# Reversing the query-tile order of every second key tile in the values product of an attention kernel

## The chip, the cores and the metric

The kernel runs on one core of a Trainium2 chip, so no other core of this program competes with it. The metric is the time of one execution on the device in microseconds (us); the median of several runs is quoted. The granted clock is the share of its full speed that TensorE was allowed; a run with a lowered clock would be slow. Times of a kernel are compared with runs of the kernel before on the same chip, made in the same rounds.

## The reference, cut to what matters

The computation is one attention block with 32 heads over a cached key and value store, gated by a SwiGLU network:

```python
xn = _layernorm(x)
q = (xn @ wq).reshape(B, Sq, H, Dh)              # Sq = 2048, H = 32, Dh = 192
scores = einsum("bhqd,bhkd->bhqk", q, k_cache) * Dh ** -0.5   # Sk = 2048
p = _softmax(scores)
o = einsum("bhqk,bhkd->bhqd", p, v_cache)        # the "values" product
s = o.reshape(B, Sq, H * Dh) @ wo
g = _silu(w2 of (silu(xn @ w1) * (xn @ w3)))
return x + s * g
```

(Shortened and re-laid; the change touches the line of `o` only.)

## The kernel before: the parts that matter

The attention is a stream of 1024 units: 32 heads x 4 blocks of 512 queries x 8 pairs of key tiles. For each unit the kernel computes the transposed scores of 256 keys and 512 queries (`st2`), takes the exponential on ScalarE into `pT2` (bf16), and multiplies by the values. The scores of unit n + 2 are issued just ahead of the values of unit n, so ScalarE has time for its work. (The code is shortened, and its comments are added here; `p` counts the 8 pairs of key tiles.)

```python
for n, (h, qb, p) in enumerate(stream):
    ...
    scores(n + 2)
    values(n)
    ...

def emit_scores(h, qb, p):          # three rounds, two row halves each
    ...
    for r, (ka, qa, kb, qb2) in enumerate(rounds):
        nc.tensor.matmul(st2[:, 0:512], lhsT=ka, rhs=qa, ...)       # rows 0..63
        nc.tensor.matmul(st2[:, 512:1024], lhsT=kb, rhs=qb2, ...)   # rows 64..127
    pT2 = pp.tile([P, 1024], BF16, tag="pT2", name="pT2")
    nc.scalar.activation(out=pT2[:], in_=st2[:], func=ACT.Exp, scale=att_scale)

vts = [vtp.tile([P, NKT, DH + 2], BF16, name=f"vt{i}") for i in range(2)]   # DH = 192

def values(n):
    h, qb, p = stream[n]
    if p == 0:
        for r in range(2):
            obanks[r] = ps_o.tile([P, 1024], F32, tag=f"ob{r}", name=f"obank{r}")
    ...
    for t in range(2):              # key tile of the unit
        for j in range(4):          # query tile of the block
            start = p == 0 and t == 0 and j % 2 == 0
            stop = p == NPAIR - 1 and t == 1 and j % 2 == 1
            for r in range(2):      # row half: keys 0..63 and 64..127 of the tile
                nc.tensor.matmul(obanks[r][:, j * 256:j * 256 + DH + 1],
                                 lhsT=pT2[r * 64:(r + 1) * 64, t * 512 + j * P:t * 512 + (j + 1) * P],
                                 rhs=vt[r * 64:(r + 1) * 64, 2 * p + t, 0:DH + 1], start=start, stop=stop)
    if p < NPAIR - 1:
        return
    ...
    nc.vector.tensor_copy(out=osum[:], in_=ov[0])
    nc.vector.tensor_tensor(out=osum[:], in0=osum[:], in1=ov[1], op=ALU.add)
```

Each matmul uses 64 of the 128 rows of the array, and the two row halves `r` write two different accumulators, `obank0` and `obank1`. An accumulator holds four query tiles, 256 fp32 columns apart; the kernel starts and stops query tiles 0 and 1 together and 2 and 3 together, and each such half of an accumulator (512 columns) is called a bank below. And a row of the values tile `vt` has 194 elements, 388 bytes, of which 193 are streamed (192 values and a column of ones that gives the softmax denominator).

## Time and profile before

| | before |
|---|---|
| time, first 3 runs | 1942.03 us (1940.68 to 1942.1) |
| profiled span | 1938.7 us, clock 0.999 |
| TensorE busy (PE) | 1929.6 us |
| ScalarE, VectorE busy | 61%, 34% |
| share of the values matmuls in the chain that ended last | 35% |

These are lines of the page of the kernel before: busy time by engine, the chain of work that ended last, and two groups of instructions. A group's columns are line, engine, operation, destination<-sources, shapes and count; then busy us and mean ns of one; then the idle time of the engine before them and what ended it. PE is TensorE's matmuls and PEld its weight loads, DVE is VectorE, ACT ScalarE and POOL GpSimd.

```profile
PE 1929.6 (100%) x27273; PEld 1318.5 (68%) x27281; DVE 654.0 (34%) x997; ACT 1180.2 (61%) x1278; POOL 282.6 (15%) x501
...
PE obank L516 35%; PE st L487 33%; PE ps L424 14%; PE ps_s L111 11%; PE ps_f L727 3%; PE ps_gu L701 1%; PE st L488 1%; DVE stats L316 0%; PE ps L410 0%; DMA x_all<-in_A_x_dram 0%; DVE xn L346 0%; PE ps L391 0%; PE pst L354 0%; DVE mv L317 0%; PE pk L271 0%
...
L516 PE MATMUL obank<-vt,pT 64*128 64x193 bf16 x16384 | 851.8, 243 | 0.0
...
L525 DVE COPY osum<-obank 128x772 f32<-128x772 f32 x128 | 123.0, 961 | 788.9 <-PE obank L516 788.9
```

PE is busy throughout and the values matmuls never wait (0.0 us of idle time before 16384 of them). "Mean 243 ns" is the length of one record, from start to a modelled end; records overlap, so it is not the pace. The pace is in the starts. This is the timeline of TensorE of the kernel before, one unit long; its columns are start us, length us, then engine, line, operation and count.

```profile
901.26 0.38 PE L487 MATMUL st<-qA,KW 64*128 64x512 bf16 x1
901.27 0.38 PE L488 MATMUL st<-qC,KW 64*128 64x512 bf16 x1
901.48 0.38 PE L487 MATMUL st<-qC,KW 64*128 64x512 bf16 x1
901.48 0.38 PE L488 MATMUL st<-qA,KW 64*128 64x512 bf16 x1
901.70 0.38 PE L487 MATMUL st<-qC,KW 64*128 64x512 bf16 x1
901.70 0.38 PE L488 MATMUL st<-qB,KW 64*128 64x512 bf16 x1
901.91 0.83 PE L516 MATMUL obank<-vt,pT 64*128 64x193 bf16 x16
902.58 0.38 PE L487 MATMUL st<-qA,KW 64*128 64x512 bf16 x1
```

The two row halves start together (901.26 and 901.27), a pair every 0.22 us for 512 columns, and the 16 values matmuls take from 901.91 to 902.58. And these are TensorE's waits of the kernel before (waiter and what it waited for: total us, times, longest us); they add up to 3.5 us in the whole run.

```profile
PE pk L569 <- POOL ident_bf masks.py:199: 2.8, 1, 2.8
PE st L487 <- ACT pT L490: 0.3, 1, 0.3
PE pst L354 <- DVE xn L346: 0.2, 1, 0.2
PE st L483 <- DVE qA L393: 0.2, 1, 0.2
```

For finer reading, the starts of single matmuls were taken from the trace and averaged over all values units that stand unmixed in it (some 1020 of 1024). A "step" is the time from the start of one pair to the start of the next. The "unit period" is the median from the start of one unit's scores to the start of the next unit's.

| kernel | steps 1 to 7 between the 8 pairs, ns | unit period, ns |
|---|---|---|
| before | 83.3, 83.3, 83.3, 83.3, **87.5**, 82.5, 82.5 | 1316 |

The fifth step, which is the time that the fifth pair takes, is 4 ns longer than its neighbours in every unit. It is called the bump below: the fifth pair is the first of the second key tile.

### The profile page before, as it was taken

How to read it: one execution, taken by the hardware profiler on the slowest of the kernel's cores; microseconds unless marked ns; L12 is line 12 of the kernel's file. 1: busy time of each engine (PE TensorE's matmuls, PEld its weight loads, DVE VectorE, ACT ScalarE, POOL GpSimd, SP SyncE). 2: the span in 40 equal slices, each digit the busy share in tenths (PEclk: the TensorE clock that was granted, in tenths of full speed). 3: DMA queues.
4: the chain of work that ended last, by engine and by line, in shares of the span. 5: the costliest groups of instructions: out<-in, count | busy, mean ns of one | idle time of the engine just before them, and what ended most of it. 6: DMA issues, size and time to landing. Idle time of an engine off the chain costs nothing.

```text
span 1938.7 us, 59672 instructions
## 1 busy us (share of the span) xinstructions
PE 1929.6 (100%) x27273; PEld 1318.5 (68%) x27281; DVE 654.0 (34%) x997; ACT 1180.2 (61%) x1278; POOL 282.6 (15%) x501
## 2 busy tenths in 40 slices
PE   9999999999999999999999999999999999999998
PEld 6666666666666666666666666666666666577776
DVE  7333333333333333333333333333333334521111
ACT  6677676767676767776767777677767677210000
POOL 3111111111111111111111111111111110000000
PEclk9999999999999999999999999999999999999999
DMA  7643433323233433353434333434333220937772
GB/s 181 129 101 67 98 68 86 83 60 88 59 89 62 99 62 98 68 162 68 101 65 100 68 101 68 101 64 100 69 71 94 57 69 2 262 67 135 152 152 61
DMA packets 394643, 178.98 MB, mean 92 GB/s; under 512 B 341616, under 2 KB 382832, under 8 KB 394384
## 3 DMA queue, kind: packets, MB, share of 16 engines
q1 hardware_dynamic: 371136, 125.32, 30.3%
q0 software_dynamic: 19472, 45.71, 9.6%
q8 instruction: 215, 3.52, 0.8%
q10 hardware_dynamic: 3776, 4.06, 0.6%
q14 instruction: 44, 0.36, 0.1%
HBM read 52.82 MB, written 27.79 MB: 42 GB/s over the span
## 4 chain that ended last, share of the span: by engine, by line
PE 98%; DVE 1%; DMA 0%; ACT 0%; issue 0%; POOL 0%; DVEq 0%; ACTq 0%
PE obank L516 35%; PE st L487 33%; PE ps L424 14%; PE ps_s L111 11%; PE ps_f L727 3%; PE ps_gu L701 1%; PE st L488 1%; DVE stats L316 0%; PE ps L410 0%; DMA x_all<-in_A_x_dram 0%; DVE xn L346 0%; PE ps L391 0%; PE pst L354 0%; DVE mv L317 0%; PE pk L271 0%
## 5 line engine op out<-in xcount | busy, mean ns | idle before, releaser
L490 ACT ACTIVATE pT<-st 128x1024 bf16<-128x1024 f32 x1024 | 1046.2, 1022 | 251.8 <-PE st L488 236.2
L516 PEld LDWEIGHTS <-pT 64*128 64x128 bf16 x16384 | 713.7, 94 | 242.2 <-ACT pT L490 0.2
L516 PE MATMUL obank<-vt,pT 64*128 64x193 bf16 x16384 | 851.8, 243 | 0.0
L487 PE MATMUL st<-qC,KW 64*128 64x512 bf16 x2046 | 605.6, 376 | 0.1
L525 DVE COPY osum<-obank 128x772 f32<-128x772 f32 x128 | 123.0, 961 | 788.9 <-PE obank L516 788.9
L488 PE MATMUL st<-qB,KW 64*128 64x512 bf16 x1024 | 385.0, 376 | 0.0
L487 PE MATMUL st<-qA,KW 64*128 64x512 bf16 x1022 | 384.3, 376 | 0.4 <-ACT pT L490 0.3
L488 PE MATMUL st<-qC,KW 64*128 64x512 bf16 x1022 | 384.3, 376 | 0.0
L488 PE MATMUL st<-qA,KW 64*128 64x512 bf16 x1022 | 384.3, 376 | 0.0
L487 PEld LDWEIGHTS <-KW 64*128 64x128 bf16 x3068 | 278.0, 94 | 153.8 <-issue 2.1
L424 PE MATMUL ps<-xnT,W 64*128 64x512 bf16 x1280 | 297.2, 376 | 0.0
L424 PE MATMUL ps<-xnS,W 64*128 64x512 bf16 x1280 | 296.3, 376 | 0.0
L488 PEld LDWEIGHTS <-KW 64*128 64x128 bf16 x3068 | 278.0, 94 | 0.7 <-issue 0.6
L377 POOL DMA_DIRECT2D qC<-qA x124 | 65.4, 528 | 1285.6 <-DVE rl_all L532 1270.0
L430 ACT CAST qB<-ps 128x512 bf16<-128x512 f32 x131 | 76.7, 586 | 228.5 <-PE ps L424 222.9
L111 PE MATMUL ps_s<-wo_sb,oT 128*128 128x384 bf16 (+3 forms) x1535 | 208.8, 299 | 0.1
L424 PEld LDWEIGHTS <-W 64*128 64x128 bf16 x2560 | 122.9, 94 | 121.2
L111 PEld LDWEIGHTS <-oT 128*128 128x128 bf16 x1536 | 148.4, 98 | 60.4
L526 DVE TENSOR_TENSOR osum<-osum,obank 128x772 f32<-128x772 f32 x128 | 122.7, 958 | 13.4
L533 DVE TENSOR_TENSOR ostage<-osum,rl_all 128x768 bf16<-128x768 f32 x128 | 122.6, 958 | 4.4
L465 DVE SCALAR_TENSOR_TENSOR hT<-pt,qB 64x512 bf16<-64x512 bf16 x64 | 43.8, 684 | 199.5 <-ACT pt L464 199.5
L429 DVE CAST qA<-ps 128x512 bf16<-128x512 f32 x131 | 90.5, 691 | 25.2 <-PE ps L410 7.3
(84 smaller groups left out, 623.8 us busy)
## 6 DMA issues: line engine op xcount, KB each, us to landing
o_scr<-ostage SPq DMA_DIRECT2D x16, 1536.0 KB, 10.0
vt<-in_A_v_cache_dram SPq DMA_DIRECT2D x63, 384.0 KB, 5.6
qC<-qA POOLq DMA_DIRECT2D x248, 64.0 KB, 1.9
qC<-qB POOLq DMA_DIRECT2D x124, 64.0 KB, 2.3
wo_sb<-in_A_wo_dram POOLq DMA_DIRECT2D x1, 7680.0 KB, 35.3
W<-in_A_wq_dram POOLq DMA_DIRECT2D x32, 160.0 KB, 3.4
W<-in_B_w_dram POOLq DMA_DIRECT2D x32, 80.0 KB, 3.1
W<-in_A_wq_dram POOLq DMA_DIRECT2D x32, 80.0 KB, 2.9
```

What stands on the lines that cost most here:

```text
L111: nc.tensor.matmul(ps[:, 0:w], lhsT=oT[:, k, :], rhs=wo_sb[:, k, c0:c1], start=(k == 0), stop=(k == OC - 1))
L377: nc.gpsimd.dma_start(out=qC[0:64, half, :], in_=qAB[half][64:P, :])
L424: nc.tensor.matmul(ps[:, r * 512:(r + 1) * 512], lhsT=W[rows, j, :], rhs=xs[rows, j // 2, qs], start=(j == 0), stop=(j == 2 * DC - 1))
L429: a = nc.vector.tensor_copy(out=qAB[0][:], in_=ps[:, 0:512])
L430: b = nc.scalar.copy(out=qAB[1][:], in_=ps[:, 512:1024])
L487: nc.tensor.matmul(st2[:, 0:512], lhsT=ka, rhs=qa, start=r == 0 and nr == 3, stop=r == nr - 1)
L488: nc.tensor.matmul(st2[:, 512:1024], lhsT=kb, rhs=qb2, start=r == 0 and nr == 3, stop=r == nr - 1)
L490: nc.scalar.activation(out=pT2[:], in_=st2[:], func=ACT.Exp, scale=att_scale)
L516: nc.tensor.matmul(obanks[r][:, j * 256:j * 256 + DH + 1], lhsT=pT2[r * 64:(r + 1) * 64, t * 512 + j * P:t * 512 + (j + 1) * P], rhs=vt[r ...
L525: nc.vector.tensor_copy(out=osum[:], in_=ov[0])
L526: nc.vector.tensor_tensor(out=osum[:], in0=osum[:], in1=ov[1], op=ALU.add)
L533: nc.vector.tensor_tensor(out=ostage[:, qb * 4:qb * 4 + 4, hg * DH:(hg + 1) * DH], in0=osum[:, :, 0:DH], in1=rl.unsqueeze(2).to_broadcast( ...
```

## The change

The intent to be read from the diff: walk the second key tile's query tiles backwards, so that the middle of a unit stays on the same query tile and the same accumulator columns, and the accumulator bank changes twice in a unit instead of four times over a unit and its seam. The `stop` flag moves with the last matmul of each bank.

```diff
         for t in range(2):
-            for j in range(4):
+            for j in (range(4), range(3, -1, -1))[t]:
                 start = p == 0 and t == 0 and j % 2 == 0
-                stop = p == NPAIR - 1 and t == 1 and j % 2 == 1
+                stop = p == NPAIR - 1 and t == 1 and j % 2 == 0
                 for r in range(2):
                     nc.tensor.matmul(obanks[r][:, j * 256:j * 256 + DH + 1],
```

## The prediction

> **What bounds the kernel now.** TensorE. The page gives PE 1929.6 us of 1938.7 us busy, and the chain of waits that ended last is 98% PE: 35% on the values matmuls (obank), about 34% on the scores matmuls (st), 14% on the projections (ps), 11% on the output products. The granted clock is 0.999. Nothing keeps PE waiting in the attention stage: its waits total about 3.4 us, nearly all before the first head; the 16384 values matmuls have 0.0 us of idle time before them.
>
> A values unit is 16 matmuls, 64 rows x 193 columns, issued as 8 pairs (two row halves, two accumulator tiles). From the starts of single matmuls in the trace: 3.4 ns between the halves of a pair, about 80 ns to the next pair, 669.0 ns per unit. The Trainium skill, "TensorE: Matmul & The Clock Gate", section "Back-to-back issue gap", gives columns / 2.4 + 2.5 ns, which for 193 is 82.9 ns, or 663 ns for 8 pairs. The trace agrees to within 6 ns a unit: the unit is bound by streaming 193 columns per pair, and no order can shorten that.
>
> **What the change removes, adds and moves.** Comparing the instruction lists of both kernels, every engine has the same number, sequence and waits. In the second key tile of each unit, weights and accumulator columns are walked 3,2,1,0 instead of 0,1,2,3. Each query tile still adds its key tiles in the same order, so the result is bit-equal. Removed: 0 us. Added: 0 us. Weights are loaded for every matmul before and after: no reload is saved.
>
> New is that in the middle of a unit two consecutive pairs add to the same accumulator columns. Would that stall? This trace says no: the output products add to one address in chains of 48, at 162 ns (384 columns), 109 ns (256) and 56 ns (128, in the last tile). 56 ns is shorter than the 83 ns between the two pairs here.
>
> One irregularity: the step from the fifth pair to the sixth takes 84 ns instead of 80 in every unit. If the reversal removed it, 4 ns x 1024 units = 4 us (0.2%) would go; if it doubled it, 4 us would come. I expect it to stay where it is, at the first pair of the second key tile, because that is where the streamed operand changes, in both orders.
>
> The evictions wait for the last matmul of a block in either order, so they do not move.
>
> **Share on the critical path.** All of the values work (35%), but its length does not change.
>
> **Prediction: 1942.0 us, range 1937 to 1947.** Chances: faster by over 2% 0.01, within 2% 0.97, slower by over 2% 0.02.
>
> **What would show each step.** Starts of single matmuls: 669 ns per unit, with the middle step (fourth to fifth pair) still 80 ns, and the bump at the same place. Chain shares: obank 35% again. Values matmul mean 243 ns, busy about 852 us.
>
> **What would make it wrong.** A stall when the row-half mode adds twice running to the same columns: every 10 ns at that point would cost 10 us in total (1024 units); 2% needs a stall of 38 ns. Or the bump being tied to the address of weights or accumulator rather than to the streamed operand, worth about 4 us either way.

## The result, and the profile after

The kernel after took 1941.35 us (median of 6 runs, 1941.08 to 1942.05) and the kernel before 1941.95 us (6 runs, 1940.68 to 1942.1). The ratio is 0.9999 with a 95% interval of 0.9986 to 1.0012: the same. (Here and below a ratio is the mean time of one kernel's fast runs over that of the other's fast runs of the same rounds, so it is not quite the ratio of the medians quoted.)

The lines of the page after that answer to those above:

```profile
PE 1929.3 (99%) x27273; PEld 1318.3 (68%) x27281; DVE 654.3 (34%) x997; ACT 1181.2 (61%) x1278; POOL 282.5 (15%) x501
...
PE obank L516 35%; PE st L487 34%; PE ps L424 14%; PE ps_s L111 11%; PE ps_f L727 3%; PE ps_gu L701 1%; PE st L488 1%; PE ps L410 0%; DVE stats L316 0%; DMA x_all<-in_A_x_dram 0%; ACT pT L490 0%; PE ps L391 0%; PE pst L354 0%; PE pk L271 0%; DVE xn L346 0%
...
L516 PE MATMUL obank<-vt,pT 64*128 64x193 bf16 x16384 | 851.8, 243 | 0.0
...
L525 DVE COPY osum<-obank 128x772 f32<-128x772 f32 x128 | 123.1, 962 | 788.7 <-PE obank L516 788.7
```

The timeline of TensorE of the kernel after, for one values unit and its neighbours:

```profile
902.26 0.38 PE L487 MATMUL st<-qC,KW 64*128 64x512 bf16 x1
902.26 0.38 PE L488 MATMUL st<-qB,KW 64*128 64x512 bf16 x1
902.48 0.83 PE L516 MATMUL obank<-vt,pT 64*128 64x193 bf16 x16
903.14 0.38 PE L487 MATMUL st<-qA,KW 64*128 64x512 bf16 x1
```

TensorE's waits of the kernel after still add up to only some 4.4 us:

```profile
PE pk L569 <- POOL ident_bf masks.py:199: 2.8, 1, 2.8
PE pst L354 <- DVE xn L346: 0.6, 1, 0.6
PE pst L354 <- ACT pT L490: 0.5, 1, 0.5
PE st L487 <- ACT pT L490: 0.3, 1, 0.3
PE st L483 <- DVE qA L393: 0.2, 1, 0.2
```

Nothing moved: the same 851.8 us of values records, no idle time before them, the same 35% of the chain, the same wait of VectorE for the end of a block (788.9 and 788.7 us). The steps after are 83.3, 83.3, 83.3, 83.3, 87.5, 82.5, 82.5 ns and the unit period is 1316 ns, equal to those before in each place.

### The profile page after: what moved, and what is told of

Same layout as the page of the kernel before. It is cut to its first block, busy times and chain, and to the rows that moved or that the text cites. A ratio compares the mean times of both kernels' runs of the same rounds, so it can differ in the third digit from the quotient of the medians.

```text
span 1939.3 us, 59672 instructions
## 1 busy us (share of the span) xinstructions
PE 1929.3 (99%) x27273; PEld 1318.3 (68%) x27281; DVE 654.3 (34%) x997; ACT 1181.2 (61%) x1278; POOL 282.5 (15%) x501
## 4 chain that ended last, share of the span: by engine, by line
PE 99%; DVE 1%; ACT 0%; DMA 0%; issue 0%; ACTq 0%; DVEq 0%
PE obank L516 35%; PE st L487 34%; PE ps L424 14%; PE ps_s L111 11%; PE ps_f L727 3%; PE ps_gu L701 1%; PE st L488 1%; PE ps L410 0%; DVE stats L316 0%; DMA x_all<-in_A_x_dram 0%; ACT pT L490 0%; PE ps L391 0%; PE pst L354 0%; PE pk L271 0%; DVE xn L346 0%
## 5 line engine op out<-in xcount | busy, mean ns | idle before, releaser
L516 PE MATMUL obank<-vt,pT 64*128 64x193 bf16 x16384 | 851.8, 243 | 0.0
L525 DVE COPY osum<-obank 128x772 f32<-128x772 f32 x128 | 123.1, 962 | 788.7 <-PE obank L516 788.7
```

The costliest lines, as they stand in the source:

```text
L516: nc.tensor.matmul(obanks[r][:, j * 256:j * 256 + DH + 1], lhsT=pT2[r * 64:(r + 1) * 64, t * 512 + j * P:t * 512 + (j + 1) * P], rhs=vt[r ...
```

## The experiments

"The same" alone doesn't show why: two effects could cancel, or the timing could be too coarse. So the experiments go to extremes of order, measure the resolution, and ask what the bump is. All were edits of the kernel before unless said otherwise, and all passed the comparison with the reference; that comparison is loose enough that the runs which are wrong on purpose pass too, probably because the attention's part of the output is small beside the residual `x` (this was not checked).

The theory: TensorE streams 193 columns per pair, and the order of query tiles does not enter. Rival 1: adding twice running to the same columns costs something, which the change balanced by removing something else. Rival 2: a change of accumulator bank has a price. Rival 3: the weight loads set the pace.

### 1. All key tiles of a query tile together (same_columns)

```diff
-        for t in range(2):
-            for j in range(4):
+        for j in range(4):
+            for t in range(2):
```

> Both key tiles of a query tile run next to each other: four pairs of neighbours per unit add to the same accumulator columns (0 before, 1 in the change), and the streamed operand changes at every pair instead of once. Theory (streaming 193 columns sets the pace, order is free): 669 ns per unit, 1941 to 1943 us. Rival 1 (adding twice running to the same columns has a cost that the change hid by removing something else): a step of over 83 ns at each of the four same-column neighbours, e.g. +5 ns each would be 20 ns x 1024 = +20 us. On the bump of 84 ns between fifth and sixth pair: if it belongs to the change of the streamed operand, as the prediction said, it should come seven times, about +6 x 4 ns x 1024 = +25 us; if it belongs to the odd key tile's rows, four times, +12 us; if it belongs to the place in the unit, once, +0.

Measured: 1947.21 us against 1941.27 us, ratio 1.0029 (1.0016 to 1.0043). Small, but clear of noise. The steps are 83.3, **87.5**, 82.5, **86.2**, 82.5, **86.1**, 82.5 ns, and the unit period is 1322 ns; (1322 - 1316) ns x 1024 units = 6.1 us, which is the whole difference. Every pair of the second key tile that these steps show is long. That fits Rival 1, as each of these pairs adds to the columns that the pair before it added to. It also fits a cost of coming from the first key tile's row to the second's, which is now paid four times. The size (+6 us) met none of the sums written beforehand. This run left the question open, and runs 6 and 7 settle it.

### 2. A bank change at every pair (banks_alternate)

```diff
-            for j in range(4):
+            for j in (0, 2, 1, 3):
```

> Query tiles in the order 0,2,1,3 in both key tiles: consecutive pairs always write different banks (bank changes at every pair; before it was every second pair). The opposite extreme to the change. Theory: nothing, 669 ns per unit, 1941 to 1943 us. Rival 2 (changing or staying in an accumulator bank has a price and the change only exchanged one for the other): the steps at bank changes differ from those within a bank; 4 more changes per unit at x ns each give 4.1 us per ns of x.

Measured: 1941.26 us against 1941.27 us, ratio 0.9999 (0.9985 to 1.0013); steps as before, the bump included. With eight bank changes instead of four, nothing changed. Rival 2 falls: banks have no price in this stream.

### 3. The second key tile first (key_tiles_swapped)

```diff
-        for t in range(2):
+        for t in (1, 0):
             for j in range(4):
-                start = p == 0 and t == 0 and j % 2 == 0
-                stop = p == NPAIR - 1 and t == 1 and j % 2 == 1
+                start = p == 0 and t == 1 and j % 2 == 0
+                stop = p == NPAIR - 1 and t == 0 and j % 2 == 1
```

> Second key tile first, then the first, query tiles forward. For the bump only: if it belongs to the rows of the odd key tile (their address), it moves from the fifth pair to the first; if to a change of the streamed operand in mid-unit or to the place in the unit, it stays between fifth and sixth pair. Time in every case 1941 to 1943 us, as the odd tile is only moved.

Measured: 1939.33 us against 1941.27 us, ratio 0.9988 (0.9974 to 1.0002). The steps are 83.3 or 83.4 ns in all seven places and the unit period is 1314 ns. The bump neither stayed nor moved to the first pair: it vanished. So it does not belong to "the streamed operand changes in mid-unit", as the prediction said, since it changes here too; nor to the place. None of the alternatives was right. What differs is the direction: from the second key tile's row to the first one's.

### 4. Two columns less (two_columns_less)

```diff
+                c0 = 2 if t == 1 else 0
...
-                    nc.tensor.matmul(obanks[r][:, j * 256:j * 256 + DH + 1],
+                    nc.tensor.matmul(obanks[r][:, j * 256 + c0:j * 256 + DH + 1],
...
-                                     rhs=vt[r * 64:(r + 1) * 64, 2 * p + t, 0:DH + 1], start=start, stop=stop)
+                                     rhs=vt[r * 64:(r + 1) * 64, 2 * p + t, c0:DH + 1], start=start, stop=stop)
```

> Wrong result on purpose: the second key tile's matmuls leave out the first 2 of 193 columns. This asks how small an effect these timings can see, and whether streaming is the bound. Theory: 2 / 2.4 = 0.83 ns per pair, 4 pairs, 1024 units: 3.4 us less, 1938 to 1939 us. Rival 3 (the pace of a pair is set by its weight loads, which stay 128 columns wide, not by streaming): no change, 1941 to 1943 us.

Measured: 1936.97 us against 1941.27 us, ratio 0.9981 (0.9967 to 0.9994). The unit period is 1312 ns instead of 1316. So a saving of some 4 ns per unit shows, both in the time and in the steps, and the theory's 3.4 us is met to within a microsecond. (About 1 ns of the 4 is not due to the columns: as the table below shows, the bump is missing in every second unit, and run 6 puts it at 2 ns per unit.) The theory's 2.4 columns per ns come out of the prediction's own steps, too: 384, 256 and 128 columns at 162, 109 and 56 ns, which is 106 ns for 256 columns.

This run also gave the clue to the bump. Leaving out two bf16 columns moves the start of the second key tile's row by 4 bytes. The steps now differ between units with an even and an odd `p` (medians, rounded to 1 ns by the trace):

| `p` of the unit | fifth step, ns | row start of key tile 0 and of key tile 1, bytes past a multiple of 16 from the tile's start |
|---|---|---|
| 0, 2, 4, 6 | 87 | 0 and 8 |
| 1, 3, 5, 7 | 82 | 8 and 0 |

The last column follows from the layout: the row of key tile 2p + t starts 388 x (2p + t) bytes into the tile, plus 4 for the columns left out of tile 1. In the kernel before these are 0 and 4 for an even `p`, and 8 and 12 for an odd one, with a bump in both.

### 5. Sixty-four columns less (sixty_four_columns_less)

The same edit with `c0 = 64 if t == 1 else 0`.

> Wrong result on purpose: the second key tile's matmuls stream 129 of 193 columns. Theory (streaming): 64 / 2.4 = 26.7 ns per pair, 4 pairs, 1024 units: 109 us less, about 1832 us. Rival 3 (weight loads, which stay the same, set the pace or come in below 193 columns): the four narrow pairs stay above 57 ns, and less than 109 us is saved; if they set the pace already, nothing is.

Measured: 1832.65 us against 1941.01 us, ratio 0.9441 (0.9427 to 0.9456), 108.4 us less. The group's line on its page, with the two shapes merged:

```profile
L517 PE MATMUL obank<-vt,pT 64*128 64x193 bf16 (+1 forms) x16384 | 861.9, 229 | 0.3 <-ACT pT L490 0.3
```

In the 383 units that stand unmixed in the trace, the wide pairs still step by 83.3 ns and the narrow ones by 59.2, 55.8 and 55.8. The unit period fell by 108 ns, against 4 x 26.7 = 107 ns expected. Time follows columns streamed, down to 129 of them. Rival 3 falls for this range.

### 6. Padded rows (values_rows_aligned)

```diff
-    vts = [vtp.tile([P, NKT, DH + 2], BF16, name=f"vt{i}") for i in range(2)]
+    vts = [vtp.tile([P, NKT, DH + 16], BF16, name=f"vt{i}") for i in range(2)]
```

> Query tiles in the old order; each row of the values tile is padded from 194 to 208 elements (416 bytes, so that every key tile's row starts on a multiple of 16 bytes from the tile's start; before, the second key tile's rows started 4 or 12 bytes past one). Theory now: the long fifth step comes from where the row of the second key tile starts, because it vanished with the key tiles swapped and came in every other unit when two columns (4 bytes) were left out. Then no step is over 84 ns, a unit takes 667 ns or less, and the time is 2 to 5 us less, 1936 to 1940 us. Rival (the bump belongs to going on from the first to the second key tile, whatever the address): the fifth step stays at 87 ns from pair start to pair start, unit 669 ns, 1941 to 1943 us.

Measured: 1938.64 us against 1941.01 us, ratio 0.9986 (0.9972 to 0.9999). All seven steps are 83.3 ns and the unit period is 1314 ns; 2 ns x 1024 = 2.0 us. The order of key tiles and the change of the streamed operand are those of the kernel before, yet the bump is gone. It belongs to where the second key tile's row starts. The group's line, to be held against 851.8 us before:

```profile
L516 PE MATMUL obank<-vt,pT 64*128 64x193 bf16 x16384 | 849.5, 243 | 0.0
```

### 7. Padded rows with both extremes of the order (aligned_same_columns, aligned_reversed)

The edit of run 6 together with that of run 1, and the edit of run 6 applied to the kernel after.

> The order of same_columns (four neighbours per unit that add to the same accumulator columns) with the padded rows. Theory: the +6 us of same_columns came from its four row switches and not from adding twice to the same columns, so with padded rows the unit takes 667 ns and the time is the same as that of values_rows_aligned, 1936 to 1940 us. Rival 1 (the second of two additions to the same columns is slowed by about 3 ns): the unit stays near 675 to 677 ns, 1944 to 1948 us.

> The change together with the padded rows. Theory: the change is free with either row length, and the pair that adds to the columns just added to (the fifth) takes 83.3 ns like all others, so 667 ns per unit and 1938 to 1940 us, as values_rows_aligned (1938.6). Rival 1 (a second addition to the same columns is slowed by a few ns, which the bump at the same place hid in the change): the fifth step stays at 86 to 88 ns and the time at 1941 to 1943 us.

Measured: aligned_same_columns 1938.82 us against 1941.01 us, ratio 0.9990 (0.9976 to 1.0004). All seven steps are 83.3 ns and the unit period is 1314 ns. The order of run 1 cost 6 us with rows of 388 bytes and costs nothing with rows of 416. (So its sum "four times, +12 us" had the right cause and twice the size: a bump of 4 ns is about half made up by the shorter steps after it, and three more of them cost 3 x 2 ns.) aligned_reversed took 1939.64 us against 1941.16 us, ratio 0.9991 (0.9977 to 1.0004), also with seven steps of 83.3 ns and 1314 ns. So four additions running to the same columns per unit, and the one of the change, are free. Rival 1 falls, and with it the last way in which two effects could have cancelled in the change.

### 8. Rows of 392 bytes (values_rows_196)

The edit of run 6 with `DH + 4` in place of `DH + 16`.

> Old order, rows of 196 elements (392 bytes): second key tile's rows start 8 bytes past a multiple of 16 from the tile's start, first key tile's rows on one. Theory (what matters is 16 bytes): the fifth step stays at 87 ns, 669 ns per unit, 1941 to 1943 us. Rival (8 bytes suffice, only starts of 4 and 12 bytes past are slow): no bump, 667 ns, 1938 to 1940 us.

Measured: 1941.25 us against 1941.16 us, ratio 0.9999 (0.9983 to 1.0014); the fifth step is 87.5 ns, as before. Starts at multiples of 8 bytes are not enough. All the kernels fit one rule of thumb: the bump comes where the row start's remainder by 16 bytes rises from one key tile to the next (0 to 4, 8 to 12, 0 to 8), and not where it falls or stays. Run 5 fits it as well: leaving out 64 columns moves the start by 128 bytes, the remainder still rises from 0 to 4 or from 8 to 12, and the first narrow step is 59.2 instead of 55.8 ns. Nor is it the direction of the address: in run 4 the address rises in every unit, but the bump is missing where the remainder falls (8 to 0). The rule was read off these runs afterwards, and why falling remainders are free is open. The remainders above are counted from the tile's start; when the kernels before and of runs 6 and 8 were built again, the compiler had put both values tiles at multiples of 64 bytes, so they are those of the addresses too. The number of 16-byte pieces that a row touches is no explanation: the 386 bytes streamed touch 25 at each of the starts 0, 4, 8 and 12.

### 9. The order of the row halves (halves_apart, halves_apart_marked, halves_eight_apart)

This was meant as a control: an order that should matter. The program issues four matmuls of one row half, then four of the other.

```diff
-            for j in range(4):
+            for r, j in [(r, j) for r in range(2) for j in range(4)]:
...
-                for r in range(2):
-                    nc.tensor.matmul(...)
+                nc.tensor.matmul(...)
```

> The order of the row halves instead of that of the query tiles: per key tile four matmuls of the first half, then four of the second. A control: is this stream sensitive to any order at all? Theory: matmuls start in program order, and only neighbours on different row halves overlap, so 14 of 16 starts are some 80 ns apart instead of 8: 6 more steps of 80 ns per unit, about +490 us, 2430 us (an estimate from the steps measured before; some of the overlap at the two seams may differ). Rival (the engine finds its overlap in any order, so order experiments on it are blind): 1941 to 1943 us.

Measured: 1941.64 us against 1941.01 us, ratio 1.0000 (0.9985 to 1.0016). The expectation of +490 us failed completely. The steps per two matmuls are as before, the bump included. To see which halves run together, the same order was run again with two columns left out of the second half, so that a record's width tells its half (one addition `c0 = 2 if r == 1 and (p > 0 or t == 1) else 0`, used as in run 4):

> Wrong result on purpose: the order of halves_apart, with the second row half streaming 191 columns instead of 193 (except once per block), so that each record in the trace tells its half. The expectation of halves_apart (+490 us) failed. Theory now: the two row halves are started as two independent streams, each in its own order, so the trace shows 193 and 191 side by side in every pair, although the program has four of one half and then four of the other. Rival (starts are in program order and something else hides the cost): the records show four of 193, then four of 191. Time about 1936 to 1942 us either way.

Measured once: 1941.3 us, state unknown. In 893 values units the widths in order of start are 193, 191, 193, 191 and so on to the end (the other 128 units found are the first of their block, where the first key tile is not marked). The first starts of one such unit, in ns from its first:

```
start    0   17   83  101  167  187  250  268  333  350
width  193  191  193  191  193  191  193  191  193  191
```

The program has the widths 193 four times, then 191 four times. So the engine starts the matmuls of the two row halves as two streams, each in its own order, and not in program order. (It is not the compiler that interleaves them: when the kernel was built again, its compiled TensorE instructions had four matmuls of 193 columns and then four of 191.) The order of the change needs none of this, as it leaves the two halves of each pair side by side in the program. How far does this reach?

```diff
-        for t in range(2):
-            for j in range(4):
+        for r in range(2):
+            for t, j in [(t, j) for t in range(2) for j in range(4)]:
```

(again marked with `c0` as above)

> Wrong result on purpose, marked in the same way: all eight matmuls of the first half, then all eight of the second. How far does the overlap of the halves reach? Theory (independent streams, no limit within 16 instructions): as before, 1936 to 1942 us, 193 and 191 side by side. Rival (the engine looks only a few instructions ahead): the second half starts late, at least some steps of 80 ns are added per unit, 4 of them being +330 us.

Measured: 1977.33 us against 1941.16 us, ratio 1.0187 (1.0171 to 1.0202): 36 us longer, some 35 ns per unit. Neither sum was met. This is its timeline of TensorE, from the last scores of one unit into the next:

```profile
903.12 0.39 PE L487 MATMUL st<-qA,KW 64*128 64x512 bf16 x1
903.19 0.33 PE L516 MATMUL obank<-vt,pT 64*128 64x191 bf16 x2
903.35 0.38 PE L487 MATMUL st<-qC,KW 64*128 64x512 bf16 x1
903.36 0.24 PE L516 MATMUL obank<-vt,pT 64*128 64x191 bf16 x1
903.44 0.38 PE L488 MATMUL st<-qC,KW 64*128 64x512 bf16 x1
903.56 0.38 PE L487 MATMUL st<-qC,KW 64*128 64x512 bf16 x1
903.66 0.38 PE L488 MATMUL st<-qA,KW 64*128 64x512 bf16 x1
903.78 0.33 PE L516 MATMUL obank<-vt,pT 64*128 64x193 bf16 x2
903.87 0.38 PE L488 MATMUL st<-qB,KW 64*128 64x512 bf16 x1
903.94 0.76 PE L516 MATMUL obank<-vt,pT 64*128 64x193 bf16 x11
```

(The last line merges both widths under the first one's.) Much of the overlap is recovered across the border of units: scores of the next unit's first half (903.12, 903.35) start while values of the second half (width 191) are still being started. How far ahead the engine reaches shows in the starts of single matmuls. In all 894 units that could be matched, the first matmul of width 191, the ninth of the unit in the program, starts 8 ns after the fifth of width 193 (5th to 95th percentile 8 to 9 ns). Likewise the first scores matmul of the next unit, the 17th from there in the program, starts 8 ns after the fifth of width 191, which is the 13th (761 units, the same percentiles); that is 105 ns after its own half's last matmul, 22 ns later than a step of 83. So in this stream a matmul that waits for its turn starts just after the one four places ahead of it in the program. With four of each half in a row, as in the two runs before, the partner lies exactly within that reach; with eight it does not, and each half loses some ns at its seams.

So the control did find an order that matters, at +1.9%, but only once the partner in the other half lies beyond that reach. What in the engine sets the reach is not shown, nor whether it counts matmuls or all instructions, as each matmul has a weight load of its own before it in the program.

## Why the prediction was right, point by point

- **TensorE bounds the kernel and streaming sets the pace of a pair: right, with one part too strong.** Taking 64 of 193 columns from half the pairs saved 108.4 us against 109 us (run 5). "No order can shorten that" was too strong: exchanging the two key tiles shortens a unit by 2 ns (run 3), though its time ratio, 0.9988, has an interval that just includes 1. From the Trainium skill's formula ("TensorE: Matmul & The Clock Gate", "Back-to-back issue gap") one estimates 82.9 ns for 193 columns; the steps without the bump are 83.3 ns. The section gives this formula for an isolated matmul and other figures for a stream with weight loads, which the prediction left out; here the formula is what fits (see the closing list). Of the 6 ns per unit between formula and trace, 2 were the bump, by the unit period of run 6.
- **Nothing added, nothing removed, same sequence and waits: right.** Both profiles have 27273 records of matmuls (a few are missing from a trace) and 27281 of weight loads, PE is busy for 1929.6 and 1929.3 us, and its waits are 3.5 and 4.4 us, none of them at the values matmuls.
- **Two additions running to the same columns do not stall: right.** The argument was an analogy, from full-row chains at 56 ns to half-row pairs at 83 ns. It held: with aligned rows, four such neighbours per unit leave every step at 83.3 ns, and so does the change itself (run 7). Run 1 alone would have misled, since its +6 us came with same-column additions but not from them.
- **The bump stays at its place: right. Its reason: wrong.** The prediction's step "because that is where the streamed operand changes" failed. With the key tiles swapped it changes too, without a bump; with rows of 416 bytes it changes in the same direction, without a bump. The runs put the start of the row, relative to 16 bytes, in its place. The change kept the order of the two key tiles, so it kept those starts, and the bump with them. That the place came out right was luck: the reason given for it would have failed in run 3. The prediction's own reserve, that the bump might be tied to an address, named the weights or the accumulator; it was the streamed operand's address.
- **The evictions do not move: right.** VectorE waits 788.9 and 788.7 us for the end of the blocks.

The reversal was therefore free for three shown reasons: bank changes have no price (run 2), same-column additions have none (run 7), and each pair's partner in the other row half stayed next to it (run 9 shows that it may even be four matmuls away).

A version that is a little faster than the kernel before: padding the rows alone (1938.64 us), at 0.14% with an interval that ends at 0.9999. That is at the edge of what the times can resolve, and far under 2%; the unit period, 1314 against 1316 ns, says the same. It was not run side by side with the kernel after. The reversal on top of it adds nothing that shows.

## What to carry to other kernels

In this stream, bound by the columns it streams and without waits, no order of the accumulations gained more than 2 us of 1941 us. Count columns, waits and matmuls before and after, and if all are the same, no change is the first guess. Then look at what an order can still move: here, steps to another row start cost 6 us (run 1) and partners eight places apart 36 us (run 9). Read the starts of single matmuls rather than their record lengths, since a 4 ns irregularity per unit is visible there and tells where the small change is. An order that correlates with a cost need not be its cause: repeat the order with the other suspect (here the row length) taken away before blaming it.

## What the Trainium skill lacked or had wrong

- "TensorE: Matmul & The Clock Gate", under "The mechanism" of its part on packing small matmuls, says of matmuls "strict FIFO, no reordering" in start and end. Here matmuls of two row halves do start out of program order: with four of one half and then four of the other in the program, the trace shows 193 and 191 columns side by side in 893 units, and the time of the same order without the marks stayed at 1941.64 us against 1941.01 us. The reach was limited to four places in the program: at eight apart the kernel took 36 us longer, and late matmuls started 8 ns after the one four places ahead. The about 4 ns per tile that the same part gives, under "Measured speedup vs the span model", agrees with the 3.4 ns measured here between the starts of the two halves in the kernel before.
- No page tells what the start address of a streamed operand costs a matmul. Here going on to a row that starts 4 or 8 bytes further past a multiple of 16 made one pair take 87.5 instead of 83.3 ns; a unit of 1314 ns without such a step takes 1316 ns with one and 1322 ns with four. "SBUF — State Buffer", in its table of specifications, says that SBUF has 16-byte cachelines and "each cross to a new line pays a penalty"; this may be the same thing, but no run here shows the mechanism, and the page does not say that contiguous rows of any start could feel it.
- "TensorE: Matmul & The Clock Gate", section "Back-to-back issue gap", gives a sustained spacing of about 81 ns per matmul at 128 columns with a weight load for each, and of about 131 ns at 512 columns. The last output tile of this kernel's trace before ran 128-column matmuls, each with its own weight load, at 56 ns from start to start, which is what the page gives for an isolated one; the 47 recorded of 512 columns in the same tile ran at 216 ns.
- No page says whether consecutive additions to the same accumulator columns stall. Here they do not, at 56 ns (128 rows, 128 columns) and at 83.3 ns (64 rows, 193 columns).
